# A smaller descriptor scratch, seventeen weight halves beside the last block, and a rearranged end, in a fused attention and expert kernel

## The chip, the cores and the metric

The kernel runs on one core of a Trainium2 chip. The metric is device time in microseconds (us). The kernel before took 671.5 us (median of three runs, 668.95 to 672.28).

## What is computed

Three stages in float32: attention with tanh-capped scores (4 batches, 12 heads, 448 rows, head size 64), a dense layer 768 to 2048 to 768 with a squared ReLU, and a soft mixture of eight experts with four slots each. Cut to what matters:

```python
scores = cap * np.tanh(scale * np.matmul(q, k.transpose(0, 1, 3, 2)) / cap)
attn = np.exp(scores - max); attn = attn / (sum + 1e-09); x = attn @ v        # 1792 x 768
r = np.maximum(x @ w_in, 0.0); x = (s * (r * r) + b) @ w_out                  # w_in 768 x 2048
logits = x @ phi                                                              # 1792 x 32 slots
slot_input = softmax_over_tokens(logits).T @ x
for e in range(E):
    slot_out[e] = np.maximum(slot_input[e] @ w1[e], 0.0) @ w2[e]              # 768 x 1024 x 768
out = softmax_over_slots(logits) @ slot_out
```

`moe_w_in` and `moe_w_out` arrive as float64 and are converted in the kernel; the experts' weights `w1` and `w2` are float32.

## The kernel before, in words

The tokens are worked on in four blocks of 448 (one batch each). TensorE first runs attention of batch 0; then `block(bi)` interleaves the dense layer of block `bi` (`hidden`, L437: sixteen column groups `fc`, 18 matmuls each into `hp` at L449) with attention of the next batch, and with `post` (L469), which turns the squared activations into `g` and accumulates the logits `L`. Weights `w_in` come as raw slices `wr` (pool `kp`, three buffers of 3 KB a partition, L354 and L420) and are split by ScalarE and VectorE into a high and a low part `ws` (`w_split`, L423 to L435). A planner in the framework orders instructions of each engine by priority; `high_priority` moves a group forward.

After block 3, `chain` (L491) closes the softmax over tokens: `lt` (logits turned, L499), its maximum and exponential (L503 to L507), idle products that fill TensorE's wait (L562), the transposes `et` (L526), the products `pt` with `g` (L538), and `acc` (L553). `tail` (L694) then does the rest: `coef` (L703 to L708), `sg` and its transposes (L710, L713), the products `si` with `w_out` (L722), `xp` (L732), the experts' first layer `hps` with `w1` (L743), and per output piece `pc` (six of 128 columns) the second layer `so` with `w2` (L765), `ss` (L795), `selB` (L797, L798) and the products `op` over all tokens (L781), copied out of PSUM (L784, L786) and stored (L788, L791).

The weights of the tail are 54 halves of 1 MB (`wt`, 8 KB a partition): `w_out` 6, `w1` 24, `w2` 24. They are loaded by SyncE's queue (SP) in order (`prefetch`, L598, DMA at L605) into a ring of buffers (`lay_halves`, L580): 14 in pool `pf`, which exist during block 3 and are loaded there behind a mark (`issue_after(self.mark)`), five in `pf2`, which need the place of `xl` and `kp` and so come after the block's last matmul, and four in `gp`, the place of `g`, free after `pt`. Each later half waits until the one that had its buffer is used (`used`, L608). In the end loop a piece needs both halves of a group before it can start, since a half holds two experts of four; the stores are issued on SP behind all loads. GpSimd (POOL) issues seven small DMAs.

```python
ring = [(pf, f"w{i}", 0) for i in range(14)] + [(pf2, f"v{i}", 0) for i in range(5)]
ring += [(self.gp, f"g{i}", h) for i in range(2) for h in range(2)]
rest = ring[:4] + ring[6:]
```

Of the kernel before, what the change touches and what calls it, by code (L numbers as in the profile page):

```python
# [7 lines left out]
F32 = mybir.dt.float32  # L8
# [48 lines left out]
class Body:  # L57
# [289 lines left out]
    def conv_units(self):  # L347
# [5 lines left out]
        def place(fc):  # L353
            return self.turns("wr", fc, 3, 0, 3 * FC - 1, [P, KC * P], F32)  # L354
# [57 lines left out]
    def w_need(self, i):  # L412
# [6 lines left out]
        else:  # L419
            self.wr[i] = self.turns("wr", i, 3, 0, 3 * FC - 1, [P, KC * P], F32)  # L420
            self.nc.sync.dma_start(self.wr[i], self.wsc[i % FC] if self.f64 else self.io["w_in"][i % FC])

    def w_split(self, i):  # L423
# [5 lines left out]
        for k in range(2):  # L429
# [3 lines left out]
            self.nc.scalar.copy(hi, u)  # L433
            self.nc.vector.tensor_sub(lo, u, hi.bitcast(F32))  # L434
# [56 lines left out]
    def chain(self, bi, L, g):  # L491
        nc, c = self.nc, self.c
        hp = self.hp
        first = bi == 0
# [20 lines left out]
        if bi == B - 1:  # L515
            self.idle_products(ls, 6)
        ln = c["tmp"][:CP, S + 4 * P:S + 5 * P].rearrange("p (a b) -> p a b", b=32)
        nc.vector.tensor_add(ln, ln_ps[:CP, :P].rearrange("p (a b) -> p a b", b=32),
                             c["pbrow"][:CP, None, :].to_broadcast([CP, NCH, 32]))
        st = hp.tile([CP, 2, NCH], F32, tag="st", bufs=1, name="st")  # L520
        nc.vector.reduce_max(st[:, 0, :], ln, axis=AX.X)
        nc.vector.tensor_sub(ln, ln, st[:, 0, :, None].to_broadcast([CP, NCH, 32]))
# [6 lines left out]
        nc.scalar.activation(ln, ln, AF.Exp)  # L529
        if first:  # L530
            nc.vector.tensor_copy(c["z"], mb[:, 3:4])
        else:
            nc.vector.scalar_tensor_tensor(c["z"], c["z"], mb[:, 2:3], mb[:, 3:4], op0=ALU.mult, op1=ALU.add)
        yield
        pt = self.bank("pt")
        for q in range(NCH):
            for f in range(4):
                nc.tensor.matmul(pt[32 * f:32 * f + 32, :], et[:, q * 32:(q + 1) * 32],  # L538
                                 g[q // 2][:CP, q % 2, 512 * f:512 * (f + 1)], start=(q == 0), stop=(q == NCH - 1))
        nc.vector.reduce_sum(st[:, 1, :], ln, axis=AX.X)  # L540
# [9 lines left out]
        if first:  # L550
            nc.vector.tensor_copy(c["acc"], pt)
        else:
# [7 lines left out]
        yield  # L560

# [18 lines left out]
    def lay_halves(self, pf, pf2):  # L580
# [9 lines left out]
    def half(self, n):  # L590
        pool, tag, h = self.seq[n]
# [23 lines left out]
    def run(self):  # L615
        nc, tc, c = self.nc, self.tc, self.c
        with ExitStack() as top:
            pool = lambda st, name, side, **k: st.enter_context(tc.tile_pool(name=name, bufs=1, side=side, **k))
            self.gp = pool(top, "gp", "left")
            with ExitStack() as mid:  # L620
# [4 lines left out]
                self.xl = pool(xls, "xl", "left")  # L625
                wps = mid.enter_context(ExitStack())
                self.kp = pool(xls, "kp", "left")
# [24 lines left out]
                pf = pool(top, "pf", "right", reuse_waits="tile")  # L652
                self.lay_halves(pf, None)
                self.block(3, None)
                xls.close()
                pf2 = pool(top, "pf2", "right", reuse_waits="tile")
                self.lay_halves(pf, pf2)
# [6 lines left out]
    def block(self, bi, atn):  # L664
# [5 lines left out]
        for grp in range(4):  # L670
# [6 lines left out]
            for k in range(12):  # L677
# [9 lines left out]
                if last and k % 3 == 0:  # L687
                    self.prefetch(min(14, 4 * grp + k // 3 + 2), True)
# [5 lines left out]
    def tail(self):  # L694
        nc, tc, io, c = self.nc, self.tc, self.io, self.c
        with ExitStack() as ctx:
# [6 lines left out]
            coef = tp_.tile([P, 4], F32, name="coef")  # L703
            nc.vector.tensor_scalar(coef[:, 0:1], c["z"], EPS, None, op0=ALU.add)
            nc.vector.reciprocal(coef[:, 0:1], coef[:, 0:1])
            nc.vector.tensor_mul(coef[:, 1:2], coef[:, 0:1], c["s"])
            nc.vector.tensor_mul(coef[:, 2:3], coef[:, 0:1], c["z"])
            nc.vector.tensor_mul(coef[:, 2:3], coef[:, 2:3], c["b"])  # L708
            sg = c["hh"][:, 1, :]
            nc.vector.tensor_scalar(sg, c["acc"], coef[:, 1:2], coef[:, 2:3], op0=ALU.mult, op1=ALU.add)  # L710
# [207 lines left out]
```

## Time and profile before

| | us |
|---|---|
| median of three runs | 671.5 |
| the profiled execution | 667.77 |
| its span, first to last instruction | 666.0 |
| PE busy | 610.1 (92%) |
| ACT busy | 410.1 (62%) |
| DVE busy | 341.8 (51%) |
| mean granted TensorE clock, share of full | 0.979 |
| hardware DMA queue: 136.07 MB, share of 16 engines | 57.0% |

The page lists busy time by engine over the whole span, but the span has three parts with different limits: a start, a long middle in which PE is nearly always busy, and a tail of some 120 us after the last block in which the DMA engines are. A stage is read from its own stretch. The profiled execution lies 3.7 us under the median; differences are made against its rows.

### The profile page before, as it was taken

How to read it: one execution, taken by the hardware profiler on the slowest of the kernel's cores; microseconds unless marked ns; L12 is line 12 of the kernel's file. 1: busy time of each engine (PE TensorE's matmuls, PEld its weight loads, DVE VectorE, ACT ScalarE, POOL GpSimd, SP SyncE). 2: the span in 40 equal slices, each digit the busy share in tenths (PEclk: the TensorE clock that was granted, in tenths of full speed). 3: DMA queues.
4: the chain of work that ended last, by engine and by line, in shares of the span. 5: the costliest groups of instructions: out<-in, count | busy, mean ns of one | idle time of the engine just before them, and what ended most of it. 6: DMA issues, size and time to landing. Idle time of an engine off the chain costs nothing.

```text
span 666.0 us, 11260 instructions
## 1 busy us (share of the span) xinstructions
PE 610.1 (92%) x4570; PEld 398.8 (60%) x4570; DVE 341.8 (51%) x497; ACT 410.1 (62%) x696; POOL 4.1 (1%) x11
## 2 busy tenths in 40 slices
PE   5878999999989999999999999999999988986863
PEld 2333575656566656566586566578878863335743
DVE  4987789788964565653533744544422222201121
ACT  6988899789866687666767759665646641000111
POOL 1000000000000000000000000000000000000000
PEclk9997999999998999999999999999999999998797
DMA  7746568586675542221421321222977639999997
GB/s 270 253 138 193 174 208 284 190 282 214 227 261 189 188 133 82 87 96 48 122 85 48 107 76 49 62 71 70 365 285 276 246 120 399 421 417 418 418 407 273
DMA packets 41419, 137.39 MB, mean 206 GB/s; under 512 B 4352, under 2 KB 15888, under 8 KB 34448
## 3 DMA queue, kind: packets, MB, share of 16 engines
q1 hardware_dynamic: 41072, 136.07, 57.0%
q8 instruction: 38, 0.62, 0.4%
q0 software_dynamic: 288, 0.53, 0.2%
q14 instruction: 21, 0.17, 0.1%
HBM read 118.49 MB, written 18.09 MB: 205 GB/s over the span
## 4 chain that ended last, share of the span: by engine, by line
PE 65%; DMA 16%; ACT 10%; DVE 5%; issue 3%; SPq 0%; DVEq 0%; ACTq 0%
PE hp L449 31%; DMA wt<-in_w_dram 11%; PE U L200 10%; PE sc L119 6%; PE tp L464 4%; DMA raw<-in_w_in_dram 2%; ACT e L165 2%; PE pt L538 2%; ACT e L123 2%; PE L L478 2%; PE tw L398 2%; PE sc L116 2%; PE Sm L183 1%; PE pp L380 1%; DVE rec L189 1%
## 5 line engine op out<-in xcount | busy, mean ns | idle before, releaser
L449 PE MATMUL hp<-x,ws 128*128 128x448 f32 x1152 | 274.9, 379 | 0.0
L449 PEld LDWEIGHTS hp<-x,ws 128*128 128x128 f32 x1152 | 206.4, 188 | 48.9 <-issue 33.5
L434 DVE TENSOR_TENSOR ws<-wr,ws 128x384 fp32r<-128x384 f32 x128 | 70.6, 555 | 120.1 <-ACT ws L433 118.6
L200 PE MATMUL U<-e,v 128*32 128x448 f32 (+1 forms) x768 | 91.9, 560 | 3.8 <-ACT e L165 1.7
L433 ACT CAST ws<-wr 128x384 fp32r<-128x384 f32 x128 | 65.6, 515 | 40.6 <-PE hp L449 40.6
L123 ACT ACTIVATE e<-sc,c_tsc 128x896 f32<-128x896 f32 x72 | 72.4, 1012 | 14.9 <-PE sc L119 14.5
L165 ACT ACTIVATE e<-e,c_acap 128x1792 f32<-128x1792 f32 (+1 forms) x48 | 77.3, 1610 | 0.7
L466 ACT COPY g<-tp 112x256 f32<-112x256 f32 x128 | 41.9, 378 | 23.3 <-PE tp L464 22.7
L200 PEld LDWEIGHTS U<-e,v 128*32 128x32 f32 (+1 forms) x768 | 23.9, 111 | 53.7 <-issue 45.6
L454 ACT ACTIVATE r<-hp 128x448 f32<-128x448 f32 x64 | 34.9, 546 | 26.4 <-PE hp L449 26.3
L119 PE MATMUL sc<-qh,kh 64*128 64x448 f32 x144 | 36.6, 483 | 13.7 <-DVE kh L76 6.4
L189 DVE RECIPROCAL rec<-rec 128x448 f32<-128x448 f32 x12 | 35.4, 2951 | 19.3 <-ACT rec L188 19.3
L765 PE MATMUL so_ps<-wt,free 128*32 128x128 f32 x768 | 29.1, 292 | 15.9 <-DMA wt<-in_w_dram 15.9
L786 ACT COPY wt<-op 128x512 f32<-128x512 f32 x12 | 7.0, 586 | 56.1 <-PE op L781 55.8
L464 PE MATMUL tp<-c_cst,r 128*112 128x128 f32 x256 | 38.9, 275 | 2.6 <-ACT g L466 1.4
L119 PEld LDWEIGHTS sc<-qh,kh 64*128 64x128 f32 x144 | 14.9, 195 | 38.7 <-issue 15.5
L455 ACT ACTIVATE r<-r 128x448 f32<-128x448 f32 x64 | 37.5, 586 | 0.4
L464 PEld LDWEIGHTS tp<-c_cst,r 128*112 128x112 f32 x256 | 29.3, 133 | 12.5 <-ACT g L466 2.7
L765 PEld LDWEIGHTS so_ps<-wt,free 128*32 128x32 f32 x768 | 23.5, 117 | 20.7 <-DMA wt<-in_w_dram 18.9
L172 DVE TENSOR_TENSOR es<-es,e 128x1792 f32<-128x1792 f32 x12 | 24.3, 2022 | 16.3 <-ACT e L165 16.3
L172 DVE TENSOR_TENSOR es<-e 128x1792 f32<-128x1792 f32 x12 | 24.3, 2023 | 15.1 <-ACT e L165 15.1
L119 PE MATMUL sc<-qh,kl 64*128 64x448 f32 x144 | 31.2, 390 | 0.6 <-DVE kl L77 0.6
(148 smaller groups left out, 639.9 us busy)
## 6 DMA issues: line engine op xcount, KB each, us to landing
wt<-in_w_dram SPq DMA_DIRECT2D x48, 1024.0 KB, 16.6
wr<-wsc SPq DMA_DIRECT2D x48, 384.0 KB, 3.1
raw<-in_w_in_dram SPq DMA_DIRECT2D x16, 768.0 KB, 5.3
raw<-in_w_outT_dram SPq DMA_DIRECT2D x16, 768.0 KB, 4.8
wsc<-wr SPq DMA_DIRECT2D x16, 384.0 KB, 2.8
osc<-o SPq DMA_DIRECT2D x24, 256.0 KB, 2.2
wt<-osc SPq DMA_DIRECT2D x6, 1024.0 KB, 6.5
k<-in_kT_dram SPq DMA_DIRECT2D x22, 256.0 KB, 3.3
```

The source lines that it names most:

```text
L119: nc.tensor.matmul(sc[:, i, :S], k[r, c * P:(c + 1) * P], q[r, :], start=(n == 0), stop=(n == 2))
L123: nc.scalar.activation(self.e[Q][c][:, 2 * j:2 * j + 2, :], sc[:, :, :S], AF.Tanh, scale=self.c["tsc"])
L165: self.nc.scalar.activation(e, e, AF.Exp, scale=self.c["acap"])
L172: self.nc.vector.tensor_add(es, e[0] if c == 1 else es, e[c])
L189: nc.vector.reciprocal(self.rec, self.rec)
L200: nc.tensor.matmul(self.U[32 * i:32 * i + 32, h, :S], self.v[2 * Q + i // 2][self.rows(i, k), d:d + 32], self.chunk(4 * Q + i, k), start=( ...
L433: self.nc.scalar.copy(hi, u)
L434: self.nc.vector.tensor_sub(lo, u, hi.bitcast(F32))
L449: nc.tensor.matmul(hp[:, :S], ws[kc // 3][:, w, kc % 3, :], x[:, s, kc, :], start=(k == 0), stop=(k == 3 * KC - 1))
L464: self.nc.tensor.transpose(tp[:CP, q * P:(q + 1) * P], r2[:, q * CP:(q + 1) * CP], self.c["idn"])
L466: self.nc.scalar.copy(self.g[q][:CP, :, fc * P:(fc + 1) * P], tp[:CP, 2 * q * P:2 * (q + 1) * P].rearrange("p (a b) -> p a b", b=P))
L765: nc.tensor.matmul(so_ps[32 * e:32 * e + 32, G, :], ht[G][:, f, 32 * e:32 * e + 32], w2[e // 2][:, e % 2, f, :], start=(f == 0), stop=(f = ...
```

## The change

Five things. The framework's descriptor scratch takes 1 KB of each SBUF partition, where it took 16 KB by default. The raw slices get a pool of their own (`wp`), closed in block 3 when the last slice is split; the ring has 15 halves in `pf`, two (`u`) in the place that this leaves, four in `pf2` and four in `gp`, 25 in all. The split of the first block's slices has a higher priority. In the last block's `chain` three idle products stand instead of six, and `coef` with its use on `acc` is computed while `pt` runs. In the end loop a half of `w2` holds four of eight row groups `f` of all four experts, so that `so` can start on one half, and `op` of the piece before stands between the two groups of a piece.

```diff
+    def raw_slice(self):
+        return self.wp.tile([P, KC * P], F32, tag="wr", bufs=3, name="wr")
...
+            with self.tc.high_priority(100) if i < FC else nullcontext():
+                self.nc.scalar.copy(hi, u)
+                self.nc.vector.tensor_sub(lo, u, hi.bitcast(F32))
...
-        if bi == B - 1:
-            self.idle_products(ls, 6)
+        if last:
+            self.idle_products(ls, 3)
...
+        if last:
+            self.coef = hp.tile([P, 4], F32, name="coef")
...
+            nc.vector.tensor_mul(k, sc, mb[:, 2:3])
+            nc.vector.tensor_scalar(c["acc"], c["acc"], k, of, op0=ALU.mult, op1=ALU.add)
...
+        elif last:
+            nc.vector.scalar_tensor_tensor(c["pw"].rearrange("p a b -> p (a b)"), pt, self.coef[:, 1:2], c["acc"], op0=ALU.mult, op1=ALU.add)
...
-        ring = [(pf, f"w{i}", 0) for i in range(14)] + [(pf2, f"v{i}", 0) for i in range(5)]
-        ring += [(self.gp, f"g{i}", h) for i in range(2) for h in range(2)]
+        ring = [(f"w{i}", 0) for i in range(15)] + [(f"u{i}", 0) for i in range(2)] + [(f"v{i}", 0) for i in range(4)]
+        ring += [(f"g{i}", h) for i in range(2) for h in range(2)]
...
                 if last and k % 3 == 0:
-                    self.prefetch(min(14, 4 * grp + k // 3 + 2), True)
+                    self.prefetch(min(15, 4 * grp + k // 3 + 2), True)
+                if last and grp == 3 and k == 6:
+                    self.wpool.close()
+                    self.halves["u"] = self.after_raw()
+                    self.prefetch(17, True)
...
-                        w2 = [self.wt.pop((k, h)).rearrange("p (e f d) -> p e f d", e=2, f=FC2) for h in range(2)]
+                    w2 = [self.wt.pop((k, h)).rearrange("p (f e d) -> p f e d", e=4, d=P) for h in range(2)]
...
+                    self.used(k)
+                    if pc and G == 0:
+                        across(pc - 1)
...
-    nc = bacc.Bacc("TRN2", target_bir_lowering=False, num_devices=1)
+    nc = bacc.Bacc("TRN2", target_bir_lowering=False, num_devices=1, dynamic_dma_scratch_size=1024)
```

SP's queue around the last raw slice (`wr` from `wsc15`), before; `wt` are halves, numbered in the order of the program:

```order
L605 DMA wt_4849<-in_w1_dram 128x2048
L421 DMA wr_4886<-wsc15_110 128x768 [waits DMAHW0_49,DVE_49]
L605 DMA wt_5000<-in_w1_dram 128x2048 [waits DMAHW7_49,PE_49]
L605 DMA wt_5002<-in_w1_dram 128x2048
L605 DMA wt_5004<-in_w1_dram 128x2048 [waits DMAHW4_49,DMAHW3_49,DMAHW6_49,DMAHW1_49,DVE_49]
L605 DMA wt_5006<-in_w1_dram 128x2048 [waits DMAHW2_49]
L605 DMA wt_5008<-in_w1_dram 128x2048 [waits PE_49,Activation_49]
```

and in the changed kernel:

```order
L632 DMA wt_4852<-in_w1_dram 128x2048
L425 DMA wr_4889<-wsc15_110 128x768 [waits DMAHW0_49,DVE_49]
L632 DMA wt_4912<-in_w1_dram 128x2048 [waits DMAHW7_49]
L632 DMA wt_4960<-in_w1_dram 128x2048 [waits DMAHW4_49,DMAHW6_49,DMAHW3_49,DVE_49]
L632 DMA wt_4962<-in_w1_dram 128x2048 [waits DMAHW1_49]
L632 DMA wt_5013<-in_w1_dram 128x2048 [waits DMAHW2_49,PE_49]
L632 DMA wt_5015<-in_w1_dram 128x2048
L632 DMA wt_5017<-in_w1_dram 128x2048
L632 DMA wt_5019<-in_w1_dram 128x2048 [waits DMAHW5_49,PE_49,Activation_49]
```

Before, the first half behind the last raw slice waits for PE. Now three stand ahead of the first one that does: the first of them waits only for an older DMA, the next two (the `u` halves) for VectorE and older DMAs.

PE at the last piece, before (`so` of the second group, then `op` of piece 4, then `ss` and `op` of piece 5):

```order
L765 MATMUL so_ps<-wt,free 32x128 [waits DMAHW5_49]
L765 MATMUL so_ps<-wt,free 32x128
L765 MATMUL so_ps<-wt,free 32x128 [waits DMAHW6_49]
L765 MATMUL so_ps<-wt,free 32x128 x29
L781 MATMUL op<-c_selB,c_ct 128x128 [waits DVE_49,Activation_49]
...
L795 MATMUL ss_ps<-c_tmp,sel 128x128 [waits DVE_49]
L795 MATMUL ss_ps<-c_tmp,sel 128x128
L781 MATMUL op<-c_selB,c_ct 128x128 [waits DVE_49,Activation_49]
L781 MATMUL op<-c_selB,c_ct 128x128 x3
```

and now:

```order
L797 MATMUL op<-c_selB,c_ct 128x128
L817 MATMUL so_ps<-wt,free 32x128 [waits DMAHW5_49]
L817 MATMUL so_ps<-wt,free 32x128 x15
L817 MATMUL so_ps<-wt,free 32x128 [waits DMAHW6_49]
L817 MATMUL so_ps<-wt,free 32x128 x15
L826 MATMUL ss_ps<-c_tmp,sel 128x128 [waits DVE_49]
L826 MATMUL ss_ps<-c_tmp,sel 128x128
L797 MATMUL op<-c_selB,c_ct 128x128 [waits DVE_49,Activation_49]
L797 MATMUL op<-c_selB,c_ct 128x128 x3
```

Behind the last half (DMAHW6) stood 30 matmuls of `so`, then all of `op` of piece 4; now 16 stand there, and `op` of piece 4 is ahead of the wait.

## Rows read from the trace of the kernel before

**Rows 1.** Page, the span in 40 slices: rate of the DMA engines

```profile
GB/s 270 253 138 193 174 208 284 190 282 214 227 261 189 188 133 82 87 96 48 122 85 48 107 76 49 62 71 70 365 285 276 246 120 399 421 417 418 418 407 273
```

**Rows 2.** Chain that ended last, 500 to 670 us: start, length, what

```profile
629.26 19.96 DMA wt<-in_w_dram
...
649.27 1.94 PE so_ps L765 x60
```

**Rows 3.** Timeline of SP's queue, 525 to 545 us: start, length, issues

```profile
525.27 0.32 SPq L421 DMA_DIRECT2D wr<-wsc  x1
542.98 2.07 SPq L605 DMA_DIRECT2D wt<-in_w_dram  x4
```

**Rows 4.** Timeline of DVE, 535 to 545 us, the last split

```profile
539.39 0.56 DVE L434 TENSOR_TENSOR ws<-wr,ws 128x384 fp32r<-128x384 f32 x1 [1.75 <-ACT ws L433]
```

**Rows 5.** Windows of 1 us: busy by engine, PE clock, DMA share, GB/s

```profile
544.00:545.00 1.00, 0.81 (x8) 0.56 (x12) 0.00 (x0) 0.26 (x2) 0.00 (x0) 1.00 1.07 180
...
557.00:558.00 1.00, 0.70 (x8) 0.39 (x4) 0.77 (x2) 0.26 (x1) 0.00 (x0) 1.00 1.08 221
558.00:559.00 1.00, 0.00 (x0) 0.00 (x0) 0.86 (x6) 0.27 (x1) 0.47 (x1) 1.00 0.74 262
```

**Rows 6.** Windows of 4 us, one in the tail

```profile
621.00:625.00 4.00, 4.00 (x28) 3.59 (x21) 1.21 (x3) 1.11 (x2) 0.00 (x0) 0.50 1.01 418
```

**Rows 7.** Timeline of PE, 545 to 562 us, the last block's chain

```profile
548.05 4.76 PE L566 MATMUL idle<-c_tmp,c_cst 128*128 128x448 f32 x12
552.74 0.40 PE L526 MATMUL et_ps<-c_cst,c_tmp 32*112 32x32 f32 x4
553.52 3.64 PE L538 MATMUL pt<-g,c_tmp 112*32 112x512 f32 x32 [0.38 <-DVE c_tmp L528]
...
560.79 1.50 PE L722 MATMUL si_ps<-wt,c_tmp 128*32 128x256 f32 x24 [0.78 <-DVE c_tmp L715]
```

**Rows 8.** Timeline of PE, 586 to 604 us, the first piece

```profile
594.36 2.16 PE L765 MATMUL so_ps<-wt,free 128*32 128x128 f32 x68
598.09 1.94 PE L765 MATMUL so_ps<-wt,free 128*32 128x128 f32 x60 [1.58 <-DMA wt<-in_w_dram]
```

**Rows 9.** Timeline of ACT, 542 to 562 us: the exponential that `et` needs

```profile
549.84 0.65 ACT L507 ACTIVATE c_tmp<-c_tmp,mb 128x448 f32<-128x448 f32 x1
```

**Rows 10.** Timeline of all engines, 640 to 666 us

```profile
649.27 1.94 PE L765 MATMUL so_ps<-wt,free 128*32 128x128 f32 x60 [2.06 <-DMA wt<-in_w_dram]
...
651.26 0.42 DVE L769 COPY c_tmp<-so_ps 128x256 f32<-128x256 f32 x1 [7.24 <-PE so_ps L765]
...
652.75 0.66 PE L795 MATMUL ss_ps<-c_tmp,sel 128*128 128x128 f32 x4
...
654.22 1.75 PE L781 MATMUL op<-c_selB,c_ct 128*128 128x128 f32 x14 [0.80 <-DVE c_selB L798]
...
655.50 3.44 SPq L788 DMA_DIRECT2D out_dram<-wt  x4
```

**Rows 11.** Windows of 1 us behind the last load

```profile
653.00:654.00 1.00, 0.41 (x4) 0.22 (x2) 0.89 (x3) 0.32 (x1) 0.00 (x0) 1.00 1.11 391
...
655.00:656.00 1.00, 0.97 (x9) 0.83 (x8) 0.66 (x1) 0.69 (x2) 0.00 (x0) 1.00 0.71 252
```

**Rows 12.** Timeline of PE, 60 to 230 us: first use of `phi`, and stalls

```profile
68.22 1.06 PE L380 MATMUL pp<-o,c_misc 128*32 128x256 f32 x12
...
88.06 1.06 PE L380 MATMUL pp<-o,c_misc 128*32 128x256 f32 x12 [0.30 <-DVE o L328]
...
198.64 0.47 PE L119 MATMUL sc<-qh,kh 64*128 64x448 f32 x2 [1.88 <-ACT e L123]
...
200.46 1.47 PE L200 MATMUL U<-e,v 128*32 128x448 f32 x2 [0.95 <-DVE x L77]
```

**Rows 13.** Timeline of POOL

```profile
3.49 0.54 POOL L840 DMA_DIRECT2D c_misc<-in_phi_dram  x1
...
558.53 0.54 POOL L702 DMA_DIRECT2D sel<-in_cst_dram  x1 [315.80 <-DVE coef L707]
```

More of the change, by code (lines that the diff above doesn't have):

```diff
@@ L493, in chain @@
         hp = self.hp
-        first = bi == 0
+        first, last = bi == 0, bi == B - 1
         ls = c["tmp"][:, 0:S]
@@ L533, in chain @@
             nc.vector.scalar_tensor_tensor(c["z"], c["z"], mb[:, 2:3], mb[:, 3:4], op0=ALU.mult, op1=ALU.add)
+        if last:
+            self.coef = hp.tile([P, 4], F32, name="coef")
+            k, sc, of = (self.coef[:, n:n + 1] for n in (0, 1, 2))
+            nc.vector.tensor_scalar(k, c["z"], EPS, None, op0=ALU.add)
+            nc.vector.reciprocal(k, k)
+            nc.vector.tensor_mul(sc, k, c["s"])
+            nc.vector.tensor_mul(of, k, c["z"])
+            nc.vector.tensor_mul(of, of, c["b"])
+            nc.vector.tensor_mul(k, sc, mb[:, 2:3])
+            nc.vector.tensor_scalar(c["acc"], c["acc"], k, of, op0=ALU.mult, op1=ALU.add)
         yield
@@ L539, in chain @@
                                  g[q // 2][:CP, q % 2, 512 * f:512 * (f + 1)], start=(q == 0), stop=(q == NCH - 1))
+        if last:
+            ln, st = self.token_logits(ln_ps)
+        nc.scalar.activation(ln, ln, AF.Exp)
         nc.vector.reduce_sum(st[:, 1, :], ln, axis=AX.X)
@@ L590, in half @@
     def half(self, n):
-        pool, tag, h = self.seq[n]
+        tag, h = self.seq[n]
+        pool = self.halves[tag[0]]
         if tag[0] != "g":
@@ L726, in tail @@
                 self.used(th)
-            free = [self.seq[n][0].tile([P, 2048], F32, tag=self.seq[n][1], bufs=1, name="free") for n in (4, 5)]
+            free = [self.halves["w"].tile([P, 2048], F32, tag=self.seq[n][0], bufs=1, name="free") for n in (4, 5)]
             xt = free[0][:, :KC * 256].rearrange("p (a b) -> p a b", b=256)
@@ new lines, in tail, with across @@
+            outs = {}
+            def across(pc):
+                gi = next(i for i, (lo, hi) in enumerate(OUT_GROUPS) if lo <= pc < hi)
+                lo, hi = OUT_GROUPS[gi]
+                if pc == lo:
+                    w = (hi - lo) * P
+                    outs[gi] = [self.half(54 + 2 * gi + h)[:, :m * w].rearrange("p (c d) -> p c d", d=w) for h, m in ((0, 8), (1, NT // P - 8))]
+                os = outs[gi]
+                dram = io["out"][:, lo * P:hi * P].rearrange("(c p) d -> p c d", p=P)
+                for q in range(0, NT // P, 4):
+                    m = min(4, NT // P - q)
+                    op = ps.tile([P, 4, P], F32, tag="A", bufs=4, name="op")
+                    for j in range(m):
+                        nc.tensor.matmul(op[:, j, :], c["ct"][:, (q + j) * P:(q + j + 1) * P], c["selB"][:, pc % 2, :], start=True, stop=True)
+                    dst = os[q // 8][:, q % 8:q % 8 + m, (pc - lo) * P:(pc - lo + 1) * P]
+                    if (q // 4) % 2:
+                        nc.vector.tensor_copy(dst, op[:, :m, :])
+                    else:
+                        nc.scalar.copy(dst, op[:, :m, :])
+                    if pc == NPC - 1:
+                        nc.sync.dma_start(dram[:, q:q + m, :], os[q // 8][:, q % 8:q % 8 + m, :])
+                if pc == hi - 1 and pc < NPC - 1:
+                    for h in range(2):
+                        nc.sync.dma_start(dram[:, 8 * h:min(8 * h + 8, NT // P), :], os[h])
@@ L801, in tile_kernel @@
+            across(NPC - 1)
 @with_exitstack
```

106 lines of the change are left out of this document (39 added, 67 removed).

## The prediction

> **What bounds the kernel now.** The first view is the page's row of 40 slices [rows 1]. From the slice at 549 us on, the DMA engines move close to 420 GB/s until the last slices; in the slice before it they move 120. So the tail runs at the rate of its loads. The chain of waits says the same: 19.96 us of it, ending at 649.27, is one stretch of waiting for weight halves, and behind that stand the last 60 matmuls of `so` [rows 2]. How much earlier that last half can land is the main question.
>
> SP's queue shows where bandwidth is lost. After the last raw slice at 525.27 nothing is issued until 542.98, when the last block's matmuls are over [rows 3]: 17.7 us in which all 14 halves allowed are already issued. From 542.98 on, 40 halves of 1.0486 MB are left. In a late window the rate is 418 GB/s [rows 6], so a half costs 1.0486/0.418 = 2.51 us, and 40 take 100 of the 106.3 us to 649.27. The rest is the start and a dip at 557 to 559, to 221 and 262 GB/s [rows 5]: the five `v` halves have landed, and the `g` places come free only when `pt` ends, at 553.52 + 3.64 = 557.16 [rows 7].
>
> Before the tail PE is the bound: it stalls six times between 60 and 220 us, from 0.30 at 88.06 to 0.95 at 200.46, 5.7 us in all, the longest 1.88 [rows 12].
>
> **The change, part by part.** *The fifteenth half.* In SP's order it stands right behind the last raw slice and no longer waits for PE's end of the block, so it is issued near 525.6, into idle engines [rows 3]. One half less behind the block: **-2.51 us**. It delays no slice, since no later one exists.
>
> *The two `u` halves.* Their place is free when the last raw slice is split. The last split on VectorE ends at 539.39 + 0.56 = 539.95 [rows 4], and it waits for TensorE, so it stays there. The stream now starts at 539.95 instead of 542.98: **-3.03 us**. That this needs 24 KB of space is what the 15 KB of scratch and 9 KB of raw slices pay for. They carry no further price on PE: no matmul waits on these engines before `si`.
>
> A rate enters the first term. The Trainium skill, page "DMA: Bandwidth & Descriptors", section Specifications, gives about 358 GB/s as one core's share of HBM; by it a half would take 2.93 us and the sum below would be 0.4 us larger. The row's 418 decides here.
>
> *The dip.* Six halves are now queued ahead of the `g` halves instead of five, and from 539.95. Before, a start at 542.98 shows 180 GB/s in the window from 544 [rows 5], so data flow some 1.5 us after an issue; six halves last until 539.95 + 1.5 + 6 x 2.51 = 556.5. `pt` itself comes earlier. Six of the twelve idle passes go, 2.38 us of 4.76 [rows 7], which would put `et` at 550.36; it also needs the exponential, over at 549.84 + 0.65 = 550.49 [rows 9]. So `et` moves from 552.74 to about 550.5, and `pt` ends at 554.9. The `g` halves are then issued 1.6 us before the queue is empty, and the dip goes: (418 - 221)/418 + (418 - 262)/418 = **-0.84 us**.
>
> *`coef` beside `pt`.* Seven small operations and one over `acc` now stand on VectorE between `et`'s copy and the end of `pt`, 3.64 us [rows 7], and fit. `si` would start some 3 us earlier than 560.79, but I cost it at **nothing**: `so` waits for halves from 598.09 on [rows 8], and PE has to be early only by then. Its cover is that wait.
>
> *The end.* Behind the last half now stand 32 passes of `so` instead of 60: 1.94 x 28/60 = 0.91 less [rows 10]. `op` of piece 4 is done before; `ss`, which started at 652.75, could have started when its input was copied, at 651.26 + 0.42 = 651.68 [rows 10], another 1.0. So the first store is issued 1.9 us earlier, counted from the last landing. Not all of this need be won, since the earlier pieces' stores run behind the loads: the engines move 391 GB/s at 653, and fall to 252 only at 655 [rows 11], when the last stores are still being issued at 655.50 [rows 10]. What can be won is the dip. It is at least 139/391 = 0.36 us in that one window, and at most the 1.9; I take **-1.0**, about the middle.
>
> *The higher priority of the first block's splits.* The changed order puts them a few places forward on ScalarE and VectorE. None of the six stalls is ended by a split, so I take **0**. Bounds: the whole 5.7 us won, or, if tanh and reciprocal are pushed back where PE waits for them, the two largest stalls doubled, +1.88 + 0.95 = +2.8 [rows 12].
>
> *The scratch.* It serves POOL's seven transfers. Their issues end at 3.49 + 0.54 = 4.03, and `phi` is first used at 68.22 [rows 12, 13]; `sel`, issued at 558.53, is used by `ss`, behind the first `so` at 594.36 [rows 8, 13]. Even if each waited for the one before it, 0.54 us of issue and a few us of flight, all is hidden. Below nothing is excluded, as nobody waits for them.
>
> **The sum.** -2.51 - 3.03 - 0.84 - 1.0 = -7.4 us. From the profiled execution's 667.8 this gives 660.4; it lies 3.7 us under the median of the three runs, 671.5, against which I predict: **664.1 us**, 1.1% less.
>
> **The rivals.** *Late `u` halves.* If the `u` loads are held until the block's end (by the mark, by a wait for more than the last split), 3.03 is lost, and with five or six halves queued from 542.98 the dip stays gone only because `pt` is earlier: 664.1 + 3.0 = 667.1. For it: SP's queue is in order, and one wait there holds all behind it. Against it: the listed order names only VectorE and older DMAs ahead of these two.
>
> *The order of the first block decides.* PE is saturated there, so whatever the new order does on PE arrives in full at the end. Gaining: 664.1 - 5.7 = 658.4. Losing: 664.1 + 2.8 = 666.9. For it: 5.7 us of stalls are there, and ScalarE's tanh ends the largest. Against: the splits move only a little, and no stall names them.
>
> *TensorE's clock falls, and PE becomes the bound of the tail (slower).* From `si` at 560.79 to `so` at 594.36 is 33.6 us with nearly no slack inside [rows 7, 8], at a clock of 1.00 in the windows around `pt` [rows 5]; in the tail one window was granted 0.50, that is 1.2 GHz instead of 2.4, where PE had been waiting for halves between short bursts [rows 6]. The three idle products removed are work that held PE busy just before that stretch. The Trainium skill, page "TensorE: Matmul & The Clock Gate", Part 1, says that the throttled state is the default and activity lifts it; by that rule, less idle work risks the clock. If the stretch ran at 1.2 GHz throughout, it would last 67 us, from 557.5 to 625. A piece costs PE two groups of 1.94, 1.75 of `op`, a copy of 0.42 and 0.66 of `ss` [rows 10], 6.7 us, against 4 x 2.51 = 10.0 of loading, so six pieces would end at 665 instead of the forecast's 642.9 for the last landing: 22 us late, 686 us. It decides from a delay of about 11 us on, since at full clock PE would be through at 557.5 + 33.6 + 6 x 6.7 = 631. Against it: the gaps of PE around `pt` become shorter with `coef` moved, not longer.
>
> *The space is not what bounds.* If the loads' rate fell with more in flight, or PE did not follow, nothing would be won but the end, 671.5 - 1.0 = 670.5. Against: the rate is flat at 420 in five slices [rows 1].
>
> **How the numbers follow.** Forecast 0.60 (661 to 667), late `u` halves 0.09, first block gaining 0.12 and losing 0.09, no gain 0.05, clock 0.05. A measurement of this kernel tells about 0.5%, 3.4 us, from no change, so faster means under 668.1. The forecast, the gaining case, nearly all of the late and the losing one fall there: 0.84. Within 0.5%: the no-gain case and the edges of two others, 0.10. Slower: the clock case and a little of what no row shows, 0.06. The range reaches from the gaining block to the losing one beside late halves: 658 to 669.
>
> **What would show it.** SP issues one half near 526 and two near 540, and four when the block ends. The DMA rate is 418 without a dip near 557; the last landing comes some 6.4 us earlier against the block's end, and the first of the last four stores 4.3 us behind it instead of 6.2. The block should end within 3 us of 542.96; if it moves more, the first block's order is the cause. If `so` no longer waits for halves, or the clock is at 0.50 from 560 on, the forecast is wrong in kind.

## The result, and the profile after

The changed kernel takes **652.27 us** (median of four runs, 651.51 to 654.73); the kernel before took 670.23 in the same session (four runs, 666.63 to 672.28). The ratio is 0.9744, 95% interval 0.9691 to 0.9797. The forecast was 664.1 with a range from 658 to 669: right in direction, but the gain is more than twice the 7.4 us forecast. Two later sessions with the same kernel gave 0.9778 and 0.9773.

The profiled execution after took 652.40 us, its span is 650.5; before, 667.77 and 666.0. The 15.5 us between the spans split at two marks that both traces have: the end of the last block's dense layer, where SP goes on before [rows 3], and the landing of the last weight half, where the last `so` starts [rows 2].

| stretch | before, us | after, us | difference | forecast |
|---|---|---|---|---|
| start to the end of block 3 | 542.98 | 535.34 | -7.64 | 0 |
| from there to the last landing | 649.27 - 542.98 = 106.29 | 635.42 - 535.34 = 100.08 | -6.21 | -6.4 |
| from there to the end of the span | 16.7 | 15.1 | -1.6 | -1.0 |

So in these two traces the tail did what was forecast, within 0.2 us, and the end a little more. What was missed lies before the tail. Two parts of the change reach into that stretch: the priority of the first block's splits, and the new places of the buffers (scratch and raw slices). The experiments tell them apart.

**The tail after.** Page, rate of the DMA engines in the 40 slices of the span, to be read against [rows 1]:

```profile
GB/s 276 229 146 208 173 212 265 213 288 243 200 282 211 182 162 78 91 93 50 110 102 48 110 53 74 39 73 49 358 262 315 317 127 422 415 419 418 418 410 307
```

The rate is as before. The chain that ended last (start, length, what) is still waiting for weight halves, for 60 us in a row, as in [rows 2]:

```profile
574.09 20.11 DMA wt<-in_w_dram
594.22 19.93 DMA wt<-in_w_dram
614.21 21.17 DMA wt<-in_w_dram
635.42 1.12 PE so_ps L817 x32
```

What changed is when the loads start. Timeline of SP's queue after, the fifteenth half and then the two `u` halves (start, length, issues):

```profile
517.59 0.32 SPq L425 DMA_DIRECT2D wr<-wsc  x1
517.96 0.42 SPq L632 DMA_DIRECT2D wt<-in_w_dram  x1
...
532.34 4.28 SPq L632 DMA_DIRECT2D wt<-in_w_dram  x5
```

Timeline of ACT after, the mark at the end of the block (the last `hp` is read):

```profile
535.34 0.54 ACT L459 ACTIVATE r<-hp 128x448 f32<-128x448 f32 x1 [1.18 <-PE hp L454]
```

The fifteenth half follows the last raw slice directly, and the stream of loads starts at 532.34, 3.00 us ahead of the block's end; the forecast had 3.03. Before, it started at that end [rows 3]. Windows of 2 us after (length, busy by engine, PE clock, DMA share, GB/s):

```profile
534.00:536.00 2.00, 1.31 (x7) 0.87 (x5) 0.00 (x0) 0.79 (x3) 0.00 (x0) 1.00 0.83 324
536.00:538.00 2.00, 1.45 (x12) 0.56 (x12) 0.00 (x0) 1.14 (x3) 0.00 (x0) 1.00 1.03 434
...
546.00:548.00 2.00, 1.96 (x20) 0.61 (x12) 0.50 (x1) 0.00 (x0) 0.00 (x0) 1.00 1.00 414
...
556.00:558.00 2.00, 2.00 (x13) 1.49 (x16) 1.43 (x3) 0.00 (x0) 0.00 (x0) 1.00 0.99 410
```

No window from 536 to 562 is under 410 GB/s: the dip to 221 and 262 [rows 5] is gone. Timeline of PE after, the last block's chain, to set against [rows 7]:

```profile
540.42 2.50 PE L592 MATMUL idle<-c_tmp,c_cst 128*128 128x448 f32 x6
543.00 0.40 PE L527 MATMUL et_ps<-c_cst,c_tmp 32*112 32x32 f32 x4
543.79 3.64 PE L548 MATMUL pt<-g,c_tmp 112*32 112x512 f32 x32 [0.38 <-DVE coef L537]
```

`et` starts 7.66 us behind the block's end (forecast 550.5 - 542.98 = 7.5), and `pt` ends 12.1 behind it, 2.1 earlier than before. Timeline of all engines at the end, against [rows 10]:

```profile
635.42 1.08 PE L817 MATMUL so_ps<-wt,free 128*32 128x128 f32 x32 [1.42 <-DMA wt<-in_w_dram]
636.57 0.42 DVE L823 COPY c_tmp<-so_ps 128x256 f32<-128x256 f32 x1 [4.01 <-PE so_ps L817]
637.05 0.71 PE L826 MATMUL ss_ps<-c_tmp,sel 128*128 128x128 f32 x4 [0.55 <-DVE c_tmp L823]
...
638.57 2.12 PE L797 MATMUL op<-c_selB,c_ct 128*128 128x128 f32 x14 [0.80 <-DVE c_selB L829]
...
639.85 4.44 SPq L804 DMA_DIRECT2D out_dram<-wt  x4
```

The first of the last stores is issued 4.43 us behind the last landing, where it was 6.23; the forecast said 4.3.

**The first block.** Here the two traces part, and within ten microseconds. PE before, two lines of its timeline around the stalls of [rows 12]:

```profile
191.16 4.78 PE L449 MATMUL hp<-x,ws 128*128 128x448 f32 x22
...
204.29 0.89 PE L449 MATMUL hp<-x,ws 128*128 128x448 f32 x3
```

and PE after:

```profile
188.34 10.68 PE L454 MATMUL hp<-x,ws 128*128 128x448 f32 x52
```

Before, no `hp` runs from 195.94 to 204.29; after, 52 run in a row. Counted through both timelines, the 264th `hp` of the program comes at 194 us in both kernels, and the 276th some 9 us later in the kernel before. Block 0 has 16 x 18 = 288 of them: the row of 52 is number 237 to 288, and before, number 273 to 288 come behind 204.29. These 16, 16 x 10.68/52 = 3.3 us of work, are what was ready to stand in the hole. The lead of 9 us is one of `hp` alone, since PE did other work meanwhile; what PE lost as a whole follows below. What holds these matmuls in the kernel before? An `hp` needs a split slice `ws`: ScalarE's copy, then VectorE's subtraction. ScalarE before, the copies:

```profile
193.56 0.92 ACT L433 CAST ws<-wr 128x384 fp32r<-128x384 f32 x2
195.57 0.51 ACT L433 CAST ws<-wr 128x384 fp32r<-128x384 f32 x1 [1.09 <-PE hp L449]
```

VectorE before, the same stretch:

```profile
191.97 2.95 DVE L189 RECIPROCAL rec<-rec 128x448 f32<-128x448 f32 x1 [2.15 <-ACT rec L188]
...
198.45 0.95 DVE L324 SCALAR_TENSOR_TENSOR o<-raw,o 128x768 int32<-128x768 int32 x1
199.32 1.08 DVE L77 TENSOR_TENSOR x<-U,x 128x896 fp32r<-128x896 f32 x1
200.32 0.95 DVE L328 SCALAR_TENSOR_TENSOR o<-raw,o 128x768 int32<-128x768 int32 x1
201.18 1.49 DVE L434 TENSOR_TENSOR ws<-wr,ws 128x384 fp32r<-128x384 f32 x3
```

Copies that ended between 194 and 196.1 wait until 201.18 for their subtraction: VectorE works without a gap on a reciprocal and eight raw conversions and products. VectorE after:

```profile
192.28 0.49 DVE L439 TENSOR_TENSOR ws<-wr,ws 128x384 fp32r<-128x384 f32 x1
...
193.15 0.55 DVE L439 TENSOR_TENSOR ws<-wr,ws 128x384 fp32r<-128x384 f32 x1
...
195.82 0.55 DVE L439 TENSOR_TENSOR ws<-wr,ws 128x384 fp32r<-128x384 f32 x1
...
199.03 0.55 DVE L439 TENSOR_TENSOR ws<-wr,ws 128x384 fp32r<-128x384 f32 x1
```

The same conversions stand between them now. Windows of 5 us, before and then after (PE's matmuls are the first number in brackets, its clock the third number from the end):

```profile
195.00:200.00 5.00, 2.63 (x17) 1.50 (x15) 5.00 (x7) 3.46 (x5) 0.00 (x0) 1.00 0.57 213
200.00:205.00 5.00, 4.54 (x18) 1.60 (x19) 4.61 (x6) 2.72 (x3) 0.00 (x0) 0.66 0.89 316
```

```profile
195.00:200.00 5.00, 5.00 (x33) 3.98 (x32) 5.00 (x8) 2.36 (x4) 0.00 (x0) 1.00 0.80 277
200.00:205.00 5.00, 5.00 (x33) 3.04 (x28) 1.51 (x3) 3.41 (x7) 0.00 (x0) 1.00 0.77 271
```

PE ran 35 matmuls before and 66 after. At 10/66 us each the 31 missing ones are 4.7 us, an estimate that takes them as equally long. The stalls of [rows 12] in that stretch, 1.88 and 0.95, make 2.83. The rest hides in the row of 200 to 205, where PE looks 91% busy: its clock is 0.66 there, and 5 x (1 - 0.66) = 1.7 us. The two together are 4.5 us. So this hole is the largest piece of the 7.64 us, but not all of it; the other 3.1 are within what executions of one kernel differ by (see the next section).

### The profile page after: what moved, and what is told of

Its sections match the earlier page's. It is cut to its first block, busy times and chain, and to the rows that moved or that the text cites. A ratio compares the mean times of both kernels' runs of the same rounds, so it can differ in the third digit from the quotient of the medians.

```text
span 650.5 us, 11248 instructions
## 1 busy us (share of the span) xinstructions
PE 599.3 (92%) x4564; PEld 391.6 (60%) x4564; DVE 341.8 (53%) x498; ACT 410.4 (63%) x696; POOL 4.1 (1%) x11
## 4 chain that ended last, share of the span: by engine, by line
PE 66%; DMA 15%; ACT 9%; DVE 6%; issue 2%; SPq 0%; DVEq 0%; ACTq 0%
PE hp L454 30%; PE U L204 10%; DMA wt<-in_w_dram 9%; PE sc L123 5%; PE tp L469 4%; PE pt L548 2%; PE hps L769 2%; DMA raw<-in_w_outT_dram 2%; PE L L483 2%; DMA raw<-in_w_in_dram 2%; PE sc L120 2%; ACT e L127 2%; ACT e L169 2%; PE tw L402 2%; PE Sm L187 1%
## 5 line engine op out<-in xcount | busy, mean ns | idle before, releaser
L204 PE MATMUL U<-e,v 128*32 128x448 f32 (+1 forms) x768 | 89.3, 554 | 3.7 <-ACT e L169 3.2
L817 PE MATMUL so_ps<-wt,free 128*32 128x128 f32 x768 | 26.2, 282 | 12.1 <-DMA wt<-in_w_dram 12.1
L817 PEld LDWEIGHTS so_ps<-wt,free 128*32 128x32 f32 x768 | 20.6, 113 | 16.3 <-DMA wt<-in_w_dram 14.2
L123 PE MATMUL sc<-ql,kh 64*128 64x448 f32 x144 | 29.9, 387 | 0.5 <-DVE ql L77 0.5
```

What stands on the lines that cost most here:

```text
L123: nc.tensor.matmul(sc[:, i, :S], k[r, c * P:(c + 1) * P], q[r, :], start=(n == 0), stop=(n == 2))
L204: nc.tensor.matmul(self.U[32 * i:32 * i + 32, h, :S], self.v[2 * Q + i // 2][self.rows(i, k), d:d + 32], self.chunk(4 * Q + i, k), start=( ...
L817: nc.tensor.matmul(so_ps[32 * e:32 * e + 32, G, :], ht[G][:, f, 32 * e:32 * e + 32], w2[f // 4][:, f % 4, e, :], start=(f == 0), stop=(f = ...
```

## The experiments

Each is compared with the kernel before in its own session (its median there was 666.1 to 668.7). "lt" is the start of the last block's `lt_ps` in the trace: before 546.48, after 538.84. A single trace gives it to some 2.5 us only. In the seven traces of kernels that have the changed kernel's code up to block 3, or all but the `u` loads (the changed kernel three times, and those below without `u`, with `u` edited, with the old end, with six idle products), lt lies from 536.42 to 541.06, the middle one at 538.84. In the three traces with the old priority it lies from 545.83 to 546.48 (the kernel before, with the small scratch, and the changed kernel without the priority).

**The priority alone, and the change without it.** In `split`, 1: the kernel before with the higher priority (two runs of the same kernel, in two sessions); 2: the changed kernel without it.

```diff
+            with self.tc.high_priority(100) if i < FC else nullcontext():
                 self.nc.scalar.copy(hi, u)
                 self.nc.vector.tensor_sub(lo, u, hi.bitcast(F32))
```

> The kernel before with one edit alone: the higher priority of the first block's splits. Theory A (the splits set the end of the first block, and the priority gave the part that the forecast missed): the last block's matmuls end near 535.5 us of the span instead of 543, and the time falls by 6 to 8 us, to a ratio of 0.988 to 0.991. Theory B (the seven microseconds came from the new pool of the raw slices, the moved addresses or the small scratch): no change, 0.998 to 1.002.

> The kernel before with the higher priority of the first block's splits alone, a second time: its first timing, 0.998 with an interval of 0.994 to 1.002, and its trace, 5.8 us shorter, do not agree. Theory A: 5 to 7 us faster, ratio 0.990 to 0.993, PE done with some 117 and 135 matmuls in the windows 180 to 200 and 200 to 220 us against 104 and 120. If the gain of the first block is given back later: the block ends early, and the tail is longer by as much; ratio 0.998.

> The changed kernel without the higher priority of the splits. Theory A: the last block's matmuls end near 543 us, and only the tail's gain of some 7.4 to 8 us is left: ratio 0.988 to 0.990. Theory B: as fast as the changed kernel, 0.974.

Without the priority the changed kernel takes 659.39 us (658.55 to 661.03), ratio 0.9836 (0.9769 to 0.9902), lt 546.12, as before. Windows of 5 us of its trace, with the hole and the clock of 0.50 behind it:

```profile
195.00:200.00 5.00, 2.08 (x12) 0.63 (x8) 5.00 (x8) 4.00 (x5) 0.00 (x0) 0.97 0.57 185
200.00:205.00 5.00, 5.00 (x22) 2.77 (x22) 3.30 (x4) 1.35 (x2) 0.00 (x0) 0.50 0.86 300
```

With the priority alone the trace of before has lt 539.18 and the same windows read

```profile
195.00:200.00 5.00, 5.00 (x33) 3.54 (x32) 5.00 (x8) 2.15 (x5) 0.00 (x0) 1.00 0.82 277
200.00:205.00 5.00, 5.00 (x30) 3.17 (x28) 0.67 (x2) 3.27 (x7) 0.00 (x0) 1.00 0.65 246
```

In time it took 665.09 (661.96 to 671.76, ten runs), ratio 0.9979 (0.9939 to 1.0019), and in the second session 664.35 (660.63 to 669.00, eleven runs), 0.9930 (0.9898 to 0.9962). So it is shown in both kernels that the priority closes the hole at 195 us. With the new places of the buffers but the old priority, lt is 546.12, so the places do not do it. By the middle traces the priority is worth 7.3 us at the last block, and single traces lie 2.5 us around that. Its worth in time is less sure in the kernel before (1.4 and 4.7 us by the ratios) than in the changed one (659.4 against 652.3 to 654.3 in three sessions, 5 to 7 us; across the sessions the fastest of the four runs without it, 658.55, is slower than the slowest of fourteen with it, 657.24).

The second profiled run of the kernel before with the priority, of 669.0 us, has lt 543.93. The hole at 195 is closed in it too, but it had lost time earlier, at a stall that the changed kernel's trace also has. That run, a stall and a window of 5 us behind it:

```profile
146.55 1.06 PE L380 MATMUL pp<-o,c_misc 128*32 128x256 f32 x12 [1.94 <-DVE o L328]
150.00:155.00 5.00, 5.00 (x22) 3.85 (x26) 0.47 (x2) 3.26 (x5) 0.00 (x0) 0.54 0.85 288
```

and the changed kernel's trace, the same two places:

```profile
145.62 1.06 PE L384 MATMUL pp<-o,c_misc 128*32 128x256 f32 x12 [1.85 <-DVE o L332]
150.00:155.00 5.00, 5.00 (x34) 3.17 (x33) 3.09 (x5) 4.68 (x7) 0.00 (x0) 1.00 0.88 274
```

Nearly the same idle time, and in one case the clock fell behind it, in the other not. In the run of 669.0 us the clock fell once more behind lt, where the idle products took 6.54 us instead of the usual 4.76.

**Which half of a split.** The priority on VectorE's subtraction only, and on ScalarE's copy only:

```diff
+            self.nc.scalar.copy(hi, u)
             with self.tc.high_priority(100) if i < FC else nullcontext():
-                self.nc.scalar.copy(hi, u)
                 self.nc.vector.tensor_sub(lo, u, hi.bitcast(F32))
```

> The changed kernel with the priority on VectorE's subtraction of a split alone, ScalarE's copy at its old priority. Theory A in the form that VectorE's subtractions were late, queued behind the reciprocal and the conversion of the raw weights: as fast as the changed kernel, 0.973 to 0.977. In the form that ScalarE's copies were late: like the kernel without the priority, 0.988.

> The changed kernel with the higher priority for ScalarE's copy of a split alone; VectorE's subtraction stands where the order without priority puts it. Theory: PE waits for the subtractions, which queue on VectorE behind the reciprocal and the raw conversions; then this is as the kernel without priority: the last block's lt_ps near 545 to 546, about 659, ratio 0.983 to 0.987. Rival: the copies are as late as the subtractions, and each of the two is half of it; then lt_ps starts near 542 to 543, about 656, ratio 0.978 to 0.982. In the windows from 180 to 220 us the first gives about 220 matmuls of hp, the second about 230, and the changed kernel 251.

The subtraction alone: 658.21 us (656.69 to 659.27), 0.9824 (0.9756 to 0.9892), lt 542.50. The copy alone: 659.59 (657.79 to 661.00), 0.9896 (0.9860 to 0.9933), lt 546.73. In time neither can be told from the change without the priority (659.39). In the first trace the hole at 195 is still there, smaller (19 and 20 matmuls, clock 0.71 in the second window). In the second, the windows from 180 to 220 hold 237 matmuls against 251, but the largest loss stands at 145 to 160, where the clock fell behind a stall of 1.93 us at 145.83, as in the run of 669.0 us above. So both halves together are needed for the gain in time; how it divides between them these two traces do not show, since one of them carries a loss that comes and goes between executions.

**The subtraction on an engine of its own.** Without the priority (1) and with it (2), the first block's subtractions on GpSimd:

```diff
-            self.nc.vector.tensor_sub(lo, u, hi.bitcast(F32))
+            (self.nc.gpsimd if i < FC else self.nc.vector).tensor_sub(lo, u, hi.bitcast(F32))
```

> The changed kernel without the priority, and in the first block the splits' subtractions on GpSimd, which is idle there, instead of on VectorE. Theory: PE waits because a subtraction stands behind the reciprocal and the conversions on VectorE; on an engine of their own they follow ScalarE's copies at once, and a large part of the priority's lead comes without any priority: lt_ps of the last block starts at 538 to 543 instead of 546.1, and the windows from 180 to 220 us show over 235 matmuls instead of 220; time 653 to 657. Rival: it is the changed order of the matmuls themselves, or ScalarE's copies, that gives the lead; then lt_ps stays near 546 and the time near 659. A price of GpSimd, where a subtraction may last longer than VectorE's 0.56 us, works against the theory.

> The changed kernel with the priority, and the first block's subtractions on GpSimd. Theory: with the priority VectorE's queue is no longer in the way, so nothing more is won: 651 to 655, ratio 0.973 to 0.979; if VectorE is still late for other work, 1 to 3 us less. If GpSimd's subtraction is slow enough to hold PE: over 656.

673.87 us (668.99 to 677.10), 1.0079 (1.0044 to 1.0114), lt 558.31; and 668.45 (665.06 to 674.53), 0.9996 (0.9959 to 1.0032), lt 557.42. The first theory and its rival both failed, by the price that the text had named; the second run came out as its last case said, over 656. Groups by form, GpSimd in the first and VectorE in the changed kernel (count, busy us, mean ns of one):

```profile
L438 POOL TENSOR_TENSOR ws<-wr,ws 128x384 fp32r<-128x384 f32 x32 | 43.2, 1352 | 159.3 <-ACT ws L437 139.2 <-PE tw L402 9.2 <-PE tp L468 7.5
```

```profile
L439 DVE TENSOR_TENSOR ws<-wr,ws 128x384 fp32r<-128x384 f32 x128 | 70.6, 554 | 117.8 <-ACT ws L438 116.3 <-DMA wr<-wsc 1.2
```

A subtraction lasts 2.4 times as long there. The 32 of them are 25.5 us longer, and lt is 12 us later than without the move, 19 in the second kernel: the first block is sensitive to its splits, but what a queue of their own would give can't be read behind that price. Whether the lead could be had from VectorE's queue alone, with the matmuls in their old order on PE, stays open, since the priority moves both.

**More of the priority.** The splits of all four blocks, and 300 in place of 100:

```diff
-            with self.tc.high_priority(100) if i < FC else nullcontext():
+            with self.tc.high_priority(100):
```

> The changed kernel with the higher priority for the splits of all four blocks, not only the first. If splits are late in the later blocks too, lt_ps of the last block starts 1 to 4 us earlier and the time is 648 to 651, ratio 0.970 to 0.974. If the later blocks' products do not wait for splits (what the runs so far suggest: nearly all of the lead of the changed kernel is there by 220 us), the same as the changed kernel, 0.974 to 0.978; if the priority pushes back the conversions or tanh of these blocks, slower, over 0.979.

> The changed kernel with the priority of the first block's splits raised from 100 to 300. If splits are still late at 100, lt_ps starts up to 2 us earlier, 650 to 652; if they are not, the same, ratio 0.974 to 0.978; if tanh and the reciprocals are pushed back now, PE stalls on them and the time is 655 to 658.

656.69 us (654.39 to 658.60, six runs), 0.9858 (0.9828 to 0.9889), lt 541.57; and 660.20 (657.84 to 662.86), 0.9881 (0.9809 to 0.9952), lt 543.61. At 300 every run is slower than each of the changed kernel's in that session (652.17 to 656.28). With all blocks the ratio lies above the three of the changed kernel, but single runs overlap with its runs, and lt is 0.5 us outside its traces. With all blocks the `hp` count is level with the changed kernel's up to 220 us or ahead of it, and falls behind from 250 us on; at 300 it is some 4.8 us behind from 260 us on, where the changed kernel's own trace of that session is level with its first. So a higher or wider priority gains nothing more, and at 300 it loses.

**The tail's space.** The ring without its two `u` halves; and their load taken out of its early place in the program:

```diff
-        ring = [(f"w{i}", 0) for i in range(15)] + [(f"u{i}", 0) for i in range(2)] + [(f"v{i}", 0) for i in range(4)]
+        ring = [(f"w{i}", 0) for i in range(15)] + [(f"v{i}", 0) for i in range(4)]
...
-                    self.prefetch(17, True)
```

> The changed kernel without its two u halves: fifteen halves are issued ahead of the block's end, and the stream behind it starts with the v halves. If the tail runs at the rate of its loads, the stream starts some 3 us later against the end of the last block, and with only four halves queued behind the fifteen the engines run dry before the g halves can be issued, about 1 to 2 us more: the last landing 3 to 5 us later against the start of lt_ps than the changed kernel's 96.2 to 96.5, the time 655 to 658, ratio 0.981 to 0.986. If the space is not what bounds: the last landing and the time as the changed kernel's, ratio 0.974 to 0.979.

> The changed kernel with the two u halves loaded when the block is over, with the v halves, instead of beside it. By the forecast's term, 3.0 us slower than the changed kernel (the last landing 3.0 us later against the block's end), ratio 0.978 to 0.982. If the engines were not what bounds the tail: as the changed kernel, 0.974.

Without them: 658.16 us (656.50 to 661.29), 0.9883 (0.9843 to 0.9924), about 1% over the changed kernel. Its lt is 539.36, and its last half lands 100.7 us behind lt, against 96.6 after: 4.2 later, where the 3.0 of the start and the dips make 3.8. This distance is steady: 96.3 to 97.0 in all ten traces of changed kernels that have the `u` halves, three idle products and a clock that stays up behind lt. Windows of 2 us:

```profile
540.00:542.00 2.00, 2.00 (x12) 1.39 (x12) 1.55 (x4) 0.00 (x0) 0.00 (x0) 1.00 0.97 320
...
548.00:550.00 2.00, 1.13 (x8) 0.68 (x8) 1.24 (x2) 0.53 (x1) 0.54 (x1) 1.00 0.90 344
```

(2 x (418 - 320)/418 + 2 x (418 - 344)/418 = 0.8). Another 2.1 us came behind the last landing, as PE ran at 1.2 GHz there; its last lines read

```profile
640.10 1.94 PE L813 MATMUL so_ps<-wt,free 128*32 128x128 f32 x32 [1.42 <-DMA wt<-in_w_dram]
...
644.61 3.22 PE L793 MATMUL op<-c_selB,c_ct 128*128 128x128 f32 x14 [0.80 <-DVE c_selB L825]
```

against 1.08 and 2.12 in the changed kernel. That low clock is not the edit's: it comes and goes at this place between traces (0.50 to 0.69 in the first 2 us behind the landing in eight of the eighteen traces, 0.98 to 1.00 in the others). The second edit delayed nothing: SP's queue issued the `u` halves at 531.43, 6.5 us ahead of lt, as in the changed kernel. So the removed line did not set the place of these loads. Its 656.71 us (651.25 to 658.95) is no test of the term; the profiled run, the one of 651.25, has the last landing 96.4 us behind lt.

**The end and the idle products.** The old loop over groups and the old layout of `w2`; and six steps of idle products instead of three:

```diff
-                    w2 = [self.wt.pop((k, h)).rearrange("p (f e d) -> p f e d", e=4, d=P) for h in range(2)]
+                    w2 = [self.wt.pop((k, h)).rearrange("p (e f d) -> p e f d", e=2, f=FC2) for h in range(2)]
...
-                    if pc and G == 0:
-                        across(pc - 1)
+                if pc:
+                    across(pc - 1)
```

```diff
-            self.idle_products(ls, 3)
+            self.idle_products(ls, 6)
```

> The changed kernel with the end loop and the layout of w2 as before: a half holds two experts, and the products over all tokens stand behind both groups of a piece. If the joined end is worth what the rows showed between the last landing and the end (16.7 us before, 15.1 in the changed kernel): 1.0 to 2.0 us slower than the changed kernel, ratio 0.976 to 0.978. If the end is bound by the stores alone: 0.974.

> The changed kernel with six idle products instead of three. pt ends 2.3 us later, near 549.7 us, and the g halves are issued so much later, but six halves are queued ahead of them until some 549.5; the forecast's view: a dip of under 1 us and the same time within 1.5 us. If PE's start of si bounds the tail: 2.3 us slower.

With the old end: 653.78 us (650.79 to 660.32), 0.9789 (0.9705 to 0.9873); in time no different from the changed kernel. In its trace the last stores are issued 6.2 us behind the last landing, as before, the span ends 16.0 behind it instead of 15.1, and the dip is back:

```profile
638.00:639.00 1.00, 1.00 (x11) 1.00 (x11) 0.04 (x1) 0.48 (x1) 0.00 (x0) 1.00 0.95 330
639.00:640.00 1.00, 0.60 (x6) 0.45 (x5) 1.00 (x2) 0.69 (x2) 0.00 (x0) 1.00 0.56 198
```

so the earlier issue, by 1.8 us, is shown: 4.4 us behind the landing in all seven traces with the new end where PE's clock was 1.00 for the first 4 us, 6.2 in both with the old. What it is worth at the end of the span is not: that comes 15.1 to 16.6 us behind the landing in the seven, and 16.0 and 16.7 behind it in the two. Six steps of idle products: 656.78 (653.53 to 658.60), 0.9834 (0.9782 to 0.9887). In its trace `pt` comes 7.05 us behind lt instead of 4.95, and the last landing 97.3 behind lt instead of 96.6: the cover of `pt` is thin, and a dip returns (250 GB/s from 548 to 550, 0.8 us). The rest of its time is not explained by that trace, which is of its fastest run.

**The scratch alone.** The kernel before with 1 KB:

```diff
-    nc = bacc.Bacc("TRN2", target_bir_lowering=False, num_devices=1)
+    nc = bacc.Bacc("TRN2", target_bir_lowering=False, num_devices=1, dynamic_dma_scratch_size=1024)
```

> The kernel before with the descriptor scratch of 1 KB alone. Forecast: no price, as nobody waits for POOL's seven transfers: ratio 0.998 to 1.002. Rival: with less scratch each of POOL's issues waits for the descriptors of the one before it to be used up, and the first block's inputs or the selection come later: POOL's issues at the start end after 4.03 us, or the time is 1 to 3 us longer.

666.84 us (664.52 to 670.01, ten runs), 1.0007 (0.9978 to 1.0036). Its fifth issue on POOL starts at 3.48 and lasts 0.54, as in [rows 13]. No price.

**The changed kernel again**, in two more sessions:

> The changed kernel once more, beside the kernel before and the three others of this call. Theory A (first block 7, tail and end 8 us): 15 to 18 us under the kernel before, ratio 0.972 to 0.978, and block 3's matmuls end near 535.5 us of the span in the trace. If the first trace was a lucky order: near 543, ratio 0.985 or above.

> The changed kernel once more, to stand beside the three others on the same chip: ratio 0.974 to 0.978 to the kernel before.

654.31 us (651.86 to 657.24, six runs), 0.9778 (0.9737 to 0.9820), and 653.38 (652.17 to 656.28), 0.9773 (0.9704 to 0.9841). The profiled run of the first, 657.24 us, shows one thing that spreads them. Its idle products on PE, and its windows of 4 us:

```profile
544.10 4.35 PE L592 MATMUL idle<-c_tmp,c_cst 128*128 128x448 f32 x6
```

```profile
540.00:544.00 4.00, 3.25 (x14) 2.10 (x10) 0.68 (x1) 0.73 (x2) 0.00 (x0) 0.63 1.01 428
544.00:548.00 4.00, 4.00 (x8) 1.92 (x7) 2.46 (x11) 1.15 (x4) 0.00 (x0) 0.52 1.00 420
548.00:552.00 4.00, 3.62 (x34) 1.23 (x36) 2.02 (x13) 0.00 (x0) 0.00 (x0) 1.00 0.79 328
```

The same six passes that took 2.50 us take 4.35 at a clock near 1.2 GHz, `pt` comes 8.1 us behind lt instead of 4.95, its `g` places come free too late, and the dip is back at 548 to 556. The trace of the second session, of 654.25 us, shows the same: 4.56 us for the six passes, `pt` 8.1 behind lt. The last halves land 98.7 and 98.0 us behind lt there, 2.2 and 1.4 later than in the first trace. So the clock fell at this place in two of the changed kernel's three traces, and the first one, which the table above rests on, is the lucky one. It fell there with six steps as well, in the run of 669.0 us above. No variant beat the changed kernel in time.

## Why the prediction was wrong, point by point

- **The failed step is "The higher priority of the first block's splits", costed at 0.** It is worth 7.3 us at the end of block 3 between the middle traces, 7.6 between the two of the table, and 5 to 7 us of time in the changed kernel. The reason given, "None of the six stalls is ended by a split", is true and does not settle the price. The label of a stall names what the next matmul in PE's order waited for, a tanh or an `x`. It does not name the 16 `hp` that stand in that place in the changed kernel; in the kernel before, their splits stood behind a reciprocal and conversions on VectorE. That the priority closes the hole is shown by the runs with and without it; that VectorE's queue is what held these `hp`, and not their place in PE's own order, is argued from the rows.
- **Its bound was wrong too.** "The whole 5.7 us won" took the idle time of PE as all there was to win. But these two stalls were followed by a stretch at a lower clock (0.66 over 5 us) in which PE counts as busy: 2.83 us of idle was 4.5 to 4.7 us of work not done, and 0.97 and 0.50 in the trace without the priority made it more. Not every stall is followed so (1.85 us at 145.62 in the changed kernel was not). The "gaining" rival, 658.4, had the right place and too small a price.
- **The fifteenth half, the `u` halves, the dip** (-2.51, -3.03, -0.84): together -6.4 forecast, -6.21 measured between the two traces. Issue right behind the last raw slice, stream 3.00 us ahead of the block's end, no dip: each as described. Taking the `u` halves away gave 4.2 us back. That it fits to 0.2 us is luck in part: in the two later traces of the same kernel the clock fell behind lt and 2.2 and 1.4 us of it were lost. The rate of 418 GB/s of the rows held, as in [rows 1, 6].
- **`coef` beside `pt`, at nothing:** held, with the cover named: `so` still waits for halves, in a chain of 60 us.
- **The end** (-1.0): -1.6 between the two traces. The stores are issued 1.8 us earlier, as forecast (1.9). The gain at the end of the span is not shown: with the clock up it ends 15.1 to 16.6 us behind the landing with the new end, 16.0 and 16.7 with the old. The bounds were 0.36 and 1.9.
- **The scratch** (0): 1.0007, held.
- **The rivals.** Late `u` halves: fell, SP issued them where the order said. Space not the bound: fell with the run without `u`. The clock as bound of the tail: no; `so` still waits for halves. But a part of that rival came true: PE's clock was 1.00 from 534 to 562 in the first trace, and near 0.5 for some 6 us behind lt in the other two, which cost 2.2 and 1.4 us. That three idle products less are the reason is not shown, since it fell there with all six too.
- **The sum with the step put right** is -7.4 - 7.6 = -15.0 us against 15.5 between the traces; since the 7.6 is taken from these traces, this says only that the other terms fit. By medians the change is 18.0 us in the first session (670.23 and 652.27; the profiled execution before lay 2.5 us under its median there, and the one after at its own), and 13.9 and 15.3 in the two later ones.

The prediction did name its own test: "The block should end within 3 us of 542.96; if it moves more, the first block's order is the cause." It moved by 7.6, and without the priority it moved back (lt 546.12).

## What to carry to other kernels

Where an engine is saturated, don't price a reordering by the labels or the idle time of its stalls: count its instructions per window in the stretch, look for ready work that could have filled the hole, and follow that work's inputs back through the queues of the other engines. A term that moves the saturated engine's inputs deserves a bound as large as the whole hole, with the stretch at a lower clock that may follow it. In the tail, by contrast, a sum over load issues and free buffers at the measured rate was right to 0.2 us in one trace and to 2.4 us in all three of the changed kernel. And take more than one trace of a kernel before reading a difference of a few us: the same code reached one place between 536.42 and 541.06.

## What the runs showed of the hardware

- Two stalls of TensorE, 1.88 and 0.95 us in the kernel before and 1.89 and 1.03 in the change without the priority, were followed by windows with a granted clock of 0.66 and 0.50: such stalls cost more than their idle time, and the busy share doesn't show it.
- A single stall of 1.94 us was followed by a window at 0.54 in one execution, and one of 1.85 us at the same place by windows at 1.00 in another: the length of a stall alone did not decide.
- The same six passes lasted 2.50, 4.35 and 4.56 us in three executions of one kernel. Granted clock around short waits explains part of a spread of some 5 us between executions.
- A 128x384 float32 subtraction took 1.352 us on GpSimd and 0.554 on VectorE.
